# Interleaving the first two output pieces of the first batch in a fused attention and GELU-MLP kernel

## The chip, the cores and the metric

The kernel runs on one core of a Trainium2 chip, in one launch. The metric is the device time of an execution in microseconds (us); the time of a kernel is the median of its runs. The core's engines are named as in the profile: PE (TensorE, the matmuls), PEld (PE's weight loads, which run beside its matmuls), DVE (VectorE), ACT (ScalarE), POOL (GpSimd) and SP (SyncE, which here only issues DMAs). Each engine takes its own instructions in the order in which the program lists them, and an instruction that waits for another engine holds all that stand behind it on its own engine.

## The reference

Cosine attention over 8 batches of 12 heads, 448 positions and 64 dimensions a head, then an exact-GELU MLP over the 3584 rows that come out:

```python
q_n = q / (norm(q) + 1e-06);  k_n = k / (norm(k) + 1e-06)
attn = softmax(q_n @ k_n.T / tau)          # per batch and head, 448 x 448
x = (attn @ v) as rows of 12 * 64 = 768    # 3584 x 768
h = x @ w_in                               # 768 x 2048
g = 0.5 * h * (1 + erf(h / sqrt(2)))
out = g @ w_out                            # 2048 x 768, float32
```

## The kernel before

A batch (448 rows of x) passes through attention in three groups of four heads, then through the first matmul of the MLP with its GELU, and then through the second, w_out. Two batches share one tile of GELU results, `g` (128 partitions, 16 rows of the hidden dimension, 896 columns), so batch 0 gives the first three output tiles of 128 columns (t = 0, 1, 2), and batch 1 the other four. The w_out work of batch b is cut into single steps that are laid between the attention steps of batch b + 1, so that PE has matmuls while ACT computes exponentials.

**An output piece.** `second_pieces(sb, t, ni)` (L414) makes the 16 steps of one piece: output tile t, half ni (384 of the 768 columns). Step kf is "row kf" of the piece: it multiplies row kf of `g` by row kf of `w_out`, in four matmuls of 64x64x384 (L427), and adds to a pair of PSUM banks, `op{sb}_{t}_{ni}`. Row 0 takes the banks (L419); row 15 is followed by their evacuation: by a DVE reduce (L436), or, where the step is run with `AC`, by a copy on ACT (L433) and an addition on DVE (L434). The evacuation stands in DVE's order at the point of the program where row 15 is recorded.

**Two bank pairs.** `free_slot()` (L410) gives the pieces pair 2 and pair 3 in turn, and each pair is one buffer. So piece 0 takes pair 2, piece 1 pair 3, piece 2 pair 2 again; the first matmul of piece 2 therefore waits until DVE has evacuated piece 0, and the first of piece 3 until piece 1 is evacuated. Pair 2 is opened by `open_third` (L385), pair 3 by `open_fourth` (L389) in the space in which the last results of the first MLP matmul lay before; its first use waits for their GELUs on ACT.

**The order.** For the first two batches the order is written out by hand in `opening()` (L538): each line records its instructions at that place, on each engine. `more(0)` (L790) appends the steps of batch 0's six pieces to a list, sorted by ni: pieces (0,0), (1,0), (2,0), (0,1), (1,1), (2,1); below they are piece 0, 1, 2 and so on. `run(n)` (L503) takes the next n steps off that list; `run(1, AC)` takes one with evacuation by ACT. With 16 steps a piece, steps 0 to 15 of the list are piece 0, steps 16 to 31 piece 1, and step 32 is row 0 of piece 2. The lines from L796 to L812 run steps 0 to 11; then come the first scores and

```python
        run(8)                              # L815: steps 12 to 19
        run(1)                              # L821: 20
        gather(3, 1)                        # L825, DVE
        run(2)                              # L826: 21, 22
        run(2)                              # L828: 23, 24
        gather(3, 2)                        # L833, DVE
        gather(3, 3)                        # L834, DVE
        run(5)                              # L835: 25 to 29
        attend(3, 4, 0)
        scores(3, ((0, 5), (1, 5)), 1)
        run(1)                              # L838: 30
        run(1, AC)                          # L839: 31
        run(5)                              # L840: 32 to 36
```

(lines without a step, a gather or the scores ahead of step 30 are left out). `scores` (L247) are matmuls, `exps` (L261) the exponentials on ACT; `gather(g, c)` (L280) adds chunk c of the exponentials to a running sum on DVE, 128x896 in float32, and waits for the exponential of its chunk.

**The weights.** `load_wo(i)` (L471) brings rows 4i to 4i + 3 of w_out, one DMA issued by POOL each; the last two of the four, for rows 8 to 11 and 12 to 15, are issued late in `opening()` (L767, L782). The first matmul of a row that comes with a new load waits for that load.

Of the kernel before, what the change touches and what calls it, by code (L numbers as in the profile page):

```python
# [16 lines left out]
def kernel(  # L17
# [25 lines left out]
    KF = d_ff // 128  # L43
# [65 lines left out]
    def pair(i, name):  # L109
        pool = late.get(i, ps_st)  # L110
        return pool.tile([128, 2, 512], F32, tag=f"st{i}", name=name)
# [290 lines left out]
    def store(sb, t, src, c0, c1, engines):  # L402
        dst = out.rearrange("(b p c) d -> b c p d", b=B, c=C)
        for h in range(2):
            bb, c = divmod(2 * t + h, C)
            engines[h].dma_start(out=dst[2 * sb + bb, c, :, c0:c1], in_=src[64 * h:64 * (h + 1)])
# [3 lines left out]
    def free_slot():  # L410
        slot[0] ^= 1
        return slot[0]

    def second_pieces(sb, t, ni):  # L414
        state = {}

        def mm(kf, eng):
            if kf == 0:
                state["ps"] = pair(free_slot(), f"op{sb}_{t}_{ni}")  # L419
                if ni == 0:  # L420
                    ot_t[sb, t] = op_.tile([128, d_model], F32, tag="ot", name=f"ot{sb}_{t}")
            ps, ot = state["ps"], ot_t[sb, t]
            for r in range(2):
                rows = slice(64 * r, 64 * (r + 1))
                for c in range(2):
                    cols = slice(64 * c, 64 * (c + 1))
                    nc.tensor.matmul(ps[cols, r, :NH], lhsT=g_t[sb][rows, kf, t * 128 + 64 * c:t * 128 + 64 * (c + 1)],  # L427
                                     rhs=wo[rows, kf, ni * NH:(ni + 1) * NH],
                                     start=(kf == 0), stop=(kf == KF - 1), tile_position=(64 * r, 64 * c))
            if kf == KF - 1:  # L430
                part = ot[:, ni * NH:(ni + 1) * NH]
                if eng is nc.scalar:
                    nc.scalar.copy(part, ps[:, 0, :NH])  # L433
                    nc.vector.tensor_tensor(part, part, ps[:, 1, :NH], ALU.add)  # L434
                else:
                    nc.vector.tensor_reduce(part, ps[:, :, :NH].rearrange("p r d -> p d r"), mybir.AxisListType.X, ALU.add)  # L436


                if sb == B // 2 - 1 and 3 <= t < 6:
                    store(sb, t, ot[:, ni * NH:(ni + 1) * NH], ni * NH, (ni + 1) * NH, (nc.sync, nc.sync))  # L440
                elif ni == 1:
                    store(sb, t, ot, 0, d_model, (nc.sync, nc.sync))

        return [lambda eng=nc.vector, kf=kf: mm(kf, eng) for kf in range(KF)]


    def last_pieces(sb, t):
        def part(c0, c1):
            ps = pair(free_slot(), f"op{sb}_{t}_{c0}")[:, 0]
            for kf in range(KF):  # L450
                nc.tensor.matmul(ps[:, :c1 - c0], lhsT=g_t[sb][:, kf, t * 128:(t + 1) * 128], rhs=wo[:, kf, c0:c1],  # L451
                                 start=(kf == 0), stop=(kf == KF - 1))
            ot = op_.tile([128, d_model], F32, tag="ot", name=f"last{c0}")[:, :c1 - c0]
            nc.vector.tensor_copy(ot, ps[:, :c1 - c0])  # L454
            store(sb, t, ot, c0, c1, (nc.sync, nc.scalar))

        n = d_model // 6
        return [lambda c0=c0, c1=c1: part(c0, c1) for c0, c1 in ((0, 3 * n), (3 * n, 5 * n), (5 * n, 6 * n))]
# [914 lines left out]
    def output_pieces(b):  # L1373
        sb, hf = divmod(b, 2)
        todo = [(t, ni) for t in (range(3) if hf == 0 else range(3, 7)) for ni in range(2)]
        if b == 0:
            todo.sort(key=lambda x: x[1])
        tail = [2 * S // 128 - 1] if b == B - 1 else []
        fill = [f for t, ni in todo if t not in tail for f in second_pieces(sb, t, ni)]
        return fill + [f for t in tail for f in last_pieces(sb, t)]  # L1380

    def more(b):
        todo_t.extend(output_pieces(b))
# [12 lines left out]
    for b in range(3, B):  # L1396
        attention(b, output_pieces(b - 1))
        first(b)
    for f in output_pieces(B - 1):
        f()  # L1400
# [35 lines left out]
```

## Time and profile before

| what | value |
|---|---|
| median of 3 runs | 391.75 us (391.03 to 391.83) |
| span of the profiled execution, first to last instruction | 390.6 us |
| what lies around the span, against the median | 1.15 us |
| DVE busy | 273.0 us, 70% of the span |
| ACT busy | 269.9 us, 69% |
| POOL busy | 248.7 us, 64% |

The profiled execution's time is its span and what lies around it, launch and end; sums are made against the 390.6 us and then added to the median. The rows of PE, and those of the stretch that the change touches (52 to 64 us after the span's start), stand in the prediction. In a row of the timeline, the first number is when the first instruction of a merged group starts, the second the time to the end of the last, and xN how many there are; consecutive PE groups overlap a little, because matmuls are pipelined.

### The profile page before, as it was taken

How to read it: one execution, taken by the hardware profiler on the slowest of the kernel's cores; microseconds unless marked ns; L12 is line 12 of the kernel's file. 1: busy time of each engine (PE TensorE's matmuls, PEld its weight loads, DVE VectorE, ACT ScalarE, POOL GpSimd, SP SyncE). 2: the span in 40 equal slices, each digit the busy share in tenths (PEclk: the TensorE clock that was granted, in tenths of full speed). 3: DMA queues.
4: the chain of work that ended last, by engine and by line, in shares of the span. 5: the costliest groups of instructions: out<-in, count | busy, mean ns of one | idle time of the engine just before them, and what ended most of it. 6: DMA issues, size and time to landing. Idle time of an engine off the chain costs nothing.

```text
span 390.6 us, 13166 instructions
## 1 busy us (share of the span) xinstructions
PE 382.6 (98%) x5820; PEld 236.6 (61%) x5820; DVE 273.0 (70%) x509; ACT 269.9 (69%) x391; POOL 248.7 (64%) x161
## 2 busy tenths in 40 slices
PE   7899999999999999999999999999999999999996
PEld 3444568555777656865567556775567555655674
DVE  4878439876778896879696896889685993670032
ACT  5895789857999958996678767997577646504300
POOL 4796950557998399969594794969595770910000
PEclk9999999999999999999999999999999999999999
DMA  8999999926899691889067490876045600130033
GB/s 265 264 262 229 176 191 329 254 56 157 179 203 299 112 217 69 185 158 275 5 172 130 120 243 2 185 131 118 3 91 81 154 9 2 44 82 2 7 79 83
DMA packets 64473, 54.85 MB, mean 140 GB/s; under 512 B 38688, under 2 KB 60320, under 8 KB 64416
## 3 DMA queue, kind: packets, MB, share of 16 engines
q1 hardware_dynamic: 54464, 41.79, 42.0%
q0 software_dynamic: 9568, 11.80, 18.5%
q8 instruction: 45, 0.74, 0.8%
q10 hardware_dynamic: 384, 0.43, 0.4%
q14 instruction: 12, 0.10, 0.1%
HBM read 45.61 MB, written 11.01 MB: 145 GB/s over the span
## 4 chain that ended last, share of the span: by engine, by line
PE 95%; DMA 2%; SPq 1%; ACT 1%; issue 0%; DVE 0%; ACTq 0%
PE hp L493 37%; PE op L427 36%; PE st L257 9%; PE o L346 8%; DMA qk<-in_k_dram 2%; PE op L451 1%; PE sm L323 1%; PE sm L332 1%; PE tp L236 1%; SPq L134 1%; ACT sq L173 0%; ACT pt L267 0%; PE spin L489 0%; DVE last L454 0%; ACT root L195 0%
## 5 line engine op out<-in xcount | busy, mean ns | idle before, releaser
L427 PE MATMUL op<-wo,g 64*64 64x384 bf16 x3456 | 167.1, 323 | 0.2 <-issue 0.2
L267 ACT ACTIVATE pt<-st 128x896 bf16<-128x896 f32 x168 | 147.2, 918 | 19.6 <-PE st L257 17.5
L493 PE MATMUL hp<-x,wi 128*128 128x448 bf16 x768 | 147.0, 353 | 0.0
L427 PEld LDWEIGHTS <-g 64*64 64x64 bf16 x3456 | 106.2, 107 | 40.9 <-issue 4.2
L493 PEld LDWEIGHTS <-wi 128*128 128x128 bf16 x768 | 74.3, 98 | 71.6 <-issue 3.2
L219 POOL TENSOR_TENSOR qkb<-qk,rn 128x896 bf16<-128x896 f32 (+1 forms) x49 | 80.4, 1662 | 46.0 <-DVE rn L203 37.9
L278 POOL TENSOR_TENSOR acc<-acc,pt 128x896 f32<-128x896 f32 x55 | 103.8, 1888 | 4.3
L436 DVE TENSOR_REDUCE ot<-op 128x384 f32<-128x768 f32 x50 | 47.3, 946 | 54.7 <-PE op L427 47.5
L1357 ACT ACTIVATE g<-hp 128x448 bf16<-128x448 f32 x96 | 46.2, 547 | 55.1 <-PE hp L493 55.1
L257 PE MATMUL st<-qkT 64*64 64x448 bf16 x672 | 62.8, 352 | 0.5 <-ACT pt L267 0.5
L183 DVE TENSOR_REDUCE nq<-sq 128x14 f32<-128x896 f32 (+1 forms) x50 | 50.4, 1036 | 13.6 <-ACT sq L173 7.1
L380 DVE TENSOR_TENSOR x<-o,rs 128x448 bf16<-128x448 f32 x48 | 27.6, 611 | 22.9 <-PE o L346 21.9
L175 POOL TENSOR_TENSOR sq<-qk 128x896 f32<-128x896 f32 x16 | 26.6, 1685 | 23.8 <-DMA qk<-in_q_dram 13.3
L346 PE MATMUL o<-pt,v 64*64 64x448 bf16 x672 | 39.5, 349 | 0.0
L290 DVE TENSOR_TENSOR acc<-acc,pt 128x896 f32<-128x896 f32 x30 | 33.0, 1099 | 1.0
L173 ACT ACTIVATE sq<-qk 128x896 f32<-128x896 f32 (+1 forms) x33 | 28.8, 901 | 4.4 <-DMA qk<-in_q_dram 3.2
L257 PEld LDWEIGHTS <-qkT 64*64 64x64 bf16 x672 | 23.1, 106 | 11.7 <-issue 3.7
L375 DVE STREAM_TRANSPOSE rs<-rc 128x448 f32<-128x448 f32 x48 | 28.1, 621 | 0.4
L278 POOL TENSOR_TENSOR acc<-pt 128x896 f32<-128x896 bf16 x11 | 20.7, 1878 | 10.9 <-ACT pt L267 10.9
L346 PEld LDWEIGHTS <-v 64*64 64x64 bf16 x672 | 21.1, 107 | 9.2 <-issue 0.2
L522 ACT ACTIVATE g<-hp 128x448 bf16<-128x448 f32 x32 | 15.4, 547 | 12.8 <-PE hp L493 12.7
L295 DVE TRANSPOSE_TENSOR_REDUCE sa<-acc 128x28 f32<-128x896 f32 x17 | 18.8, 1104 | 0.2
(54 smaller groups left out, 176.0 us busy)
## 6 DMA issues: line engine op xcount, KB each, us to landing
qk<-in_q_dram SPq DMA_DIRECT2D x23, 448.0 KB, 4.9
qk<-in_k_dram SPq DMA_DIRECT2D x23, 448.0 KB, 5.8
out_dram<-ot SPq DMA_DIRECT2D x48, 192.0 KB, 4.0
v<-in_v_dram POOLq DMA_DIRECT2D x6, 672.0 KB, 7.2
wo<-in_moe_w_out_dram POOLq DMA_DIRECT2D x4, 768.0 KB, 10.6
wi<-in_moe_w_in_dram POOLq DMA_DIRECT2D x4, 512.0 KB, 13.8
out_dram<-ot SPq DMA_DIRECT2D x12, 96.0 KB, 2.1
wi<-in_moe_w_in_dram POOLq DMA_DIRECT2D x4, 256.0 KB, 14.1
```

The costliest lines, as they stand in the source:

```text
L173: eng.activation(sq, t, AF.Square)
L183: nc.vector.tensor_reduce(nq_t[n][:, j, i], sq_t[g, i][:, s0:s1], mybir.AxisListType.X, ALU.add)
L219: eng.tensor_tensor(qkb[:, i, :, s0:s1].rearrange("p c s d -> p s c d"), t[:, i, s0:s1], rn[:, i].to_broadcast([128, s1 - s0, C, D]), ALU. ...
L257: nc.tensor.matmul(st[cols, n, :S], lhsT=qkT[rows, 1, c, cols], rhs=qkT[rows, 0, :, cols], start=True, stop=True, tile_position=(64 * s, 6 ...
L267: nc.scalar.activation(pt, st[:, :, :S], AF.Exp, scale=inv_tau)
L278: nc.gpsimd.tensor_tensor(acc_t[g], all_t[g][:, 0] if c == 1 else acc_t[g], all_t[g][:, c], ALU.add)
L290: nc.vector.tensor_tensor(acc_t[g], acc_t[g], all_t[g][:, c], ALU.add)
L346: nc.tensor.matmul(bank_t[g, h][cols, :S], lhsT=v_t[g][rows, s, c, :], rhs=pt_t[g, s, c][rows], start=(c == 0), stop=(c == C - 1), tile_po ...
L427: nc.tensor.matmul(ps[cols, r, :NH], lhsT=g_t[sb][rows, kf, t * 128 + 64 * c:t * 128 + 64 * (c + 1)], rhs=wo[rows, kf, ni * NH:(ni + 1) * NH],
L436: nc.vector.tensor_reduce(part, ps[:, :, :NH].rearrange("p r d -> p d r"), mybir.AxisListType.X, ALU.add)
L493: nc.tensor.matmul(t, lhsT=wi[:, kd, m * 128:(m + 1) * 128], rhs=x_t[b][:, kd, :], start=(kd == 0), stop=(kd == KD - 1))
L1357: nc.scalar.activation(g_t[sb][:, m, hf * S:(hf + 1) * S], hps.pop(m), AF.Gelu)
```

## The change

In batch 0 the 32 steps of pieces 0 and 1 are put in another order: rows 0 to 11 of piece 0, rows 0 to 11 of piece 1, rows 12 to 15 of piece 0, rows 12 to 15 of piece 1. The steps of the other pieces, and all lines of `opening()`, stay. The same instructions are recorded; none is added or removed.

```diff
         tail = [2 * S // 128 - 1] if b == B - 1 else []
-        fill = [f for t, ni in todo if t not in tail for f in second_pieces(sb, t, ni)]
+        pieces = [second_pieces(sb, t, ni) for t, ni in todo if t not in tail]
+        if b == 0:
+            n = KF * 3 // 4
+            one, two = pieces[:2]
+            pieces[:2] = [one[:n] + two[:n] + one[n:] + two[n:]]
+        fill = [f for p in pieces for f in p]
         return fill + [f for t in tail for f in last_pieces(sb, t)]
```

By the list, piece 0's row 15, with its evacuation, goes from step 15 to step 27; row 12 of piece 0 from step 12 to step 24; row 0 of piece 1 from step 16 to step 12. Row 15 of piece 1 stays at step 31, and row 0 of piece 2 at step 32.

On DVE, at the end of the first MLP matmul and the start of batch 1's attention (`op_0_0` and `op_1_0` are the banks of pieces 0 and 1, `op_2_0` those of piece 2, `ot_t` the output tiles in SBUF, `acc` the running sum of `gather`, `pt` the exponentials), the order before is

```order
L241 COPY qkT_754<-tp_0_763 128x896 [waits PE_49]
L436 TENSOR_REDUCE ot_0_830<-op_0_0_829 128x384 [waits PE_49,Activation_49]
L283 TENSOR_TENSOR acc_962<-pt_939 128x896 [waits Activation_49]
L283 TENSOR_TENSOR acc_962<-acc_962,pt_939 128x896 [waits DVE_49,Activation_49] x2
L434 TENSOR_TENSOR ot_1_922<-ot_1_922,op_1_0_921 128x384 [waits Activation_49]
L283 TENSOR_TENSOR acc_962<-acc_962,pt_939 128x896 [waits DVE_49]
```

and in the change

```order
L241 COPY qkT_754<-tp_0_763 128x896 [waits PE_49]
L283 TENSOR_TENSOR acc_961<-pt_938 128x896 [waits Activation_49]
L283 TENSOR_TENSOR acc_961<-acc_961,pt_938 128x896 [waits DVE_49,Activation_49] x2
L436 TENSOR_REDUCE ot_0_830<-op_0_0_829 128x384 [waits PE_49]
L434 TENSOR_TENSOR ot_1_905<-ot_1_905,op_1_0_904 128x384 [waits Activation_49]
L283 TENSOR_TENSOR acc_961<-acc_961,pt_938 128x896 [waits DVE_49]
```

The reduce that empties piece 0's banks has moved from ahead of the first three additions of `gather` to behind them. (The numbers at the ends of names are the program's counters and mean nothing.)

On PE, behind the second scores of group 3 (step 12 of the list), the order before is

```order
L257 MATMUL st_1_899<-qkT_754 64x448
L427 LDWEIGHTS g_123
L427 MATMUL op_0_0_829<-wo,g_123 64x384 [waits DMASW5_49]
L427 LDWEIGHTS g_123
L427 MATMUL op_0_0_829<-wo,g_123 64x384
```

and in the change

```order
L257 MATMUL st_1_899<-qkT_754 64x448
L427 LDWEIGHTS g_123
L427 MATMUL op_1_0_904<-wo,g_123 64x384 [waits Activation_49]
L427 LDWEIGHTS g_123
L427 MATMUL op_1_0_904<-wo,g_123 64x384
```

The row that waits for the last load of w_out (`DMASW5_49`) has left this place, to step 24, and the first row of piece 1 with its wait for ACT has come.

On PE, where piece 2 begins (steps 31 and 32), the change has

```order
L427 MATMUL op_1_0_904<-wo,g_123 64x384
L427 LDWEIGHTS g_123
L427 MATMUL op_1_0_904<-wo,g_123 64x384
L427 LDWEIGHTS g_123
L427 MATMUL op_2_0_1035<-wo,g_123 64x384 [waits DVE_49]
```

These rows read the same before, apart from counters, and nothing moved here. The wait on DVE is for the reduce of piece 0, whose banks piece 2 takes: the count of DVE instructions that it waits for is 66 before and 69 in the change.

## The prediction

> **What bounds the kernel now.** I read the page's totals first, then its chain of work that ended last, then PE's waits from 60 us on. From the page:
>
> ```profile
> span 390.6 us, 13166 instructions
> PE 382.6 (98%) x5820; PEld 236.6 (61%) x5820; DVE 273.0 (70%) x509; ACT 269.9 (69%) x391; POOL 248.7 (64%) x161
> PE 95%; DMA 2%; SPq 1%; ACT 1%; issue 0%; DVE 0%; ACTq 0%
> ```
>
> PE is busy for 382.6 of 390.6 us and holds 95% of the chain. Its waits in the window from 60 us to the end come to one row:
>
> ```profile
> PE op L427 <- issue: 0.2, 1, 0.2
> ```
>
> So behind the place of the change PE waits for 0.2 us in all. Two things follow. Time is won only by taking away a wait of PE, of which there is almost none left; and a wait that is put in is paid in full, because no later slack of PE can take it up. The question is therefore which waits of PE the change takes out or puts in between 52 and 64 us.
>
> PE's timeline of that stretch, before:
>
> ```profile
> 51.95 2.15 PE L427 MATMUL op<-wo,g 64*64 64x384 bf16 x48
> 53.93 0.55 PE L257 MATMUL st<-qkT 64*64 64x448 bf16 x8
> 54.31 1.47 PE L427 MATMUL op<-wo,g 64*64 64x384 bf16 x32
> 55.61 0.36 PE L257 MATMUL st<-qkT 64*64 64x448 bf16 x4
> 55.80 0.66 PE L427 MATMUL op<-wo,g 64*64 64x384 bf16 x12
> 56.28 0.36 PE L257 MATMUL st<-qkT 64*64 64x448 bf16 x4
> 56.47 1.31 PE L427 MATMUL op<-wo,g 64*64 64x384 bf16 x28
> 57.61 0.57 PE L257 MATMUL st<-qkT 64*64 64x448 bf16 x8
> 57.99 1.81 PE L427 MATMUL op<-wo,g 64*64 64x384 bf16 x40
> 59.61 0.38 PE L257 MATMUL st<-qkT 64*64 64x448 bf16 x4
> 59.80 1.98 PE L427 MATMUL op<-wo,g 64*64 64x384 bf16 x44
> ```
>
> Counted in steps of four matmuls, these are steps 0 to 11, 12 to 19, 20 to 22, 23 to 29, 30 to 39 and 40 to 50. No row carries an idle time. Forty matmuls (steps 30 to 39) start between 57.99 and 59.61, so a step takes 1.62 / 10 = 0.162 us. Step 32, row 0 of piece 2, starts at 57.99 + 2 x 0.162 = **58.31 us**.
>
> **What the change removes.** Row 12 of piece 0, which waits for the last load of w_out, leaves step 12. The rows of the last two loads (in the window 40 to 60 us, and the first of the two alone, in 42.5 to 43.5 us):
>
> ```profile
> L473 POOL DMA_DIRECT2D wo<-in_moe_w_out_dram x2: 760/784/808, 42.9 to 43.7; - x2
> DMA to landing us min/median/max: 7.3/8.8/10.3
> ...
> wo<-in_moe_w_out_dram POOLq DMA_DIRECT2D x1, 768.0 KB, 7.3
> ```
>
> The first took 7.3 us to land, so the last took 10.3: 43.7 + 10.3 = 54.0 us. Step 12 starts at 54.31, and PE is not idle ahead of it. In the profiled execution the load was there 0.3 us early, and the removed wait is worth **nothing**. In a timed run it could be worth something, if the load is later there. A bound from rows: all that lies between the span (390.6) and the median (391.75) is 1.15 us, so if the profile was lucky by all of that, the change wins 1.15 us. I take zero, as the row shows it. In its new place, step 24, the row starts about 56.47 + 0.16 = 56.63, and the load has landed 2.6 us earlier.
>
> **What comes to step 12.** Row 0 of piece 1 waits for ACT, whose last GELU stands in this row:
>
> ```profile
> 49.79 2.81 ACT L522 ACTIVATE g<-hp 128x448 bf16<-128x448 f32 x6 [0.59 <-PE hp L493]
> ```
>
> It ends at 52.60, 1.7 us before step 12: no cost. ACT, POOL and SP keep their order, with the same DMAs at the same places; they cost nothing by themselves.
>
> **What moves on DVE.** Piece 0's reduce goes behind three additions of `gather`. DVE's timeline before:
>
> ```profile
> 55.25 0.96 DVE L436 TENSOR_REDUCE ot<-op 128x384 f32<-128x768 f32 x1 [6.96 <-ACT pt L267]
> 56.12 1.08 DVE L283 TENSOR_TENSOR acc<-pt 128x896 f32<-128x896 bf16 x1
> 57.31 2.29 DVE L283 TENSOR_TENSOR acc<-acc,pt 128x896 f32<-128x896 f32 x2
> 59.51 0.55 DVE L434 TENSOR_TENSOR ot<-ot,op 128x384 f32<-128x384 f32 x1
> 59.98 2.28 DVE L283 TENSOR_TENSOR acc<-acc,pt 128x896 f32<-128x896 f32 x2
> 62.17 0.55 DVE L434 TENSOR_TENSOR ot<-ot,op 128x384 f32<-128x384 f32 x1
> ```
>
> Before, the reduce lay at 55.25 to 56.21, in time in which DVE had been idle (6.96 us ahead of it), and step 32 at 58.31 found the banks free 2.1 us early. In the change:
>
> 1. Do the additions start earlier without the reduce? The first waits for the second exponential. ACT's and POOL's rows:
>
> ```profile
> 54.34 3.40 ACT L267 ACTIVATE pt<-st 128x896 bf16<-128x896 f32 x4 [0.43 <-PE st L257]
> 56.13 1.13 POOL L161 COPY then<-pt 128x1 bf16<-128x1 bf16 x1 [4.25 <-ACT pt L267]
> ```
>
> POOL's copy of the same chunk starts at 56.13, just as it is released by ACT, beside the addition at 56.12. So ACT set that time and the additions stay where they are. The third ends at 57.31 + 2.29 = 59.60.
>
> 2. The reduce starts behind it. The instruction that stood there before (L434) started at 59.51, 0.09 us ahead of the addition's end, as DVE lets a next instruction that needs nothing of it begin. From 59.51 it takes 0.96 us: until **60.47**. Were it to wait for the end as the additions wait for each other (57.31 against an end at 57.20, 0.1 us later), it would be 60.66; I take the nearer row, L434.
>
> 3. From DVE's end to PE's start: in the opening PE waits for a DVE copy, in these rows of DVE (window 10.8 to 11.1 us) and PE:
>
> ```profile
> 10.70 0.55 DVE L241 COPY qkT<-tp 64x896 bf16<-64x896 bf16 x1
> 11.31 0.35 PE L489 MATMUL spin<-g,ident 128*128 128x448 bf16 x1 [0.94 <-DVE qkT L241]
> ```
>
> The copy ends at 11.25 and PE starts at 11.31: 0.06 us. Step 32 starts at 60.47 + 0.06 = **60.53**.
>
> 4. PE's new wait: 60.53 - 58.31 = **2.2 us** (2.4 with the later start). All of steps 32 onwards, scores 6 of group 3 and all of the rest stand behind it.
>
> **Is it paid again, or paid back, behind that?** Piece 1's addition follows at about 60.4 to 60.9 (0.87 us later than before), and the fourth and fifth additions of `gather` end at about 63.1 instead of 62.26. Step 48 needs piece 1's banks: before it started at 59.80 + 8 x 0.162 = 61.1, now at 63.3, with the banks free at 60.9. Piece 2's ACT copy is released by PE and goes 2.2 us later, as does everything that PE releases; its DVE addition, 62.17 before, was held by DVE itself and comes some 1.9 us later, less than PE's shift. So DVE keeps up, nothing more is paid. And by the row of PE's waits 0.2 us is all that could be won back.
>
> The sum: 390.6 + 2.2 = 392.8 for the span, and on the median 391.75 + 2.2 = **394.0 us** (0.56%).
>
> **A rule against it.** The Trainium skill, "Perfetto Trace Analysis", section "Matmuls", says that independent matmul groups should rotate through different PSUM banks, so that evacuating one overlaps the matmuls of the next. The change fills both bank pairs to the end before either is emptied. By that rule alone the price would be the evacuation as far as it finds no matmuls beside it, the first rival below. No row of before shows the exposed case.
>
> **The rivals.**
>
> *Only the bare evacuation shows.* If the reduce began as soon as piece 0's row 15 is done, DVE being free, the wait would be small. Before, row 15 of piece 0 (step 15) started at 54.31 + 3 x 0.162 = 54.80 and the reduce at 55.25, 0.45 later. In the change it is step 27, at 56.47 + 4 x 0.162 = 57.12; reduce 57.57 to 58.53, PE at 58.59, a wait of 0.3 us: **392.0 us**. For it speaks that DVE's instruction could be ready; against it that the additions stand ahead of it in DVE's order and occupy DVE from 56.12 to 59.60.
>
> *The last load of w_out is late in the timed runs.* This is the case on the other side. Place: step 12. If the load lands later than 54.31, the kernel before waits there for the excess and the change does not. It breaks even when the load lands 2.2 us after 54.31, at 56.5, and wins from there. For it speaks the margin of only 0.3 us and a landing that differs by 3 us between two equal loads; against it that runs differ by 0.8 us in all. With the bound of 1.15 us, the time is 391.75 + 2.2 - 1.15 = **392.8 us**; at break-even 391.75.
>
> *The wait costs the clock too.* PE's rows in the opening:
>
> ```profile
> 1.95 3.52 PE L489 MATMUL spin<-g,ident 128*128 128x448 bf16 x9 [1.95 <-DVE root L93]
> 5.98 1.68 PE L489 MATMUL spin<-g,ident 128*128 128x448 bf16 x8
> ```
>
> Equal matmuls take 3.52 / 9 = 0.39 us at first and 1.68 / 8 = 0.21 later, so a slow phase of about ten matmuls costs some 10 x 0.18 = 1.8 us. If an idle 2.2 us brings it back, the time is **395.8 us**. Against it: behind the idle 0.94 us ahead of 11.31 a matmul of the same shape lasted 0.35 us in all, less than the 0.39 us by which the slow ones follow each other; but no idle time of 2.2 us is shown. The Trainium skill, "TensorE: Matmul & The Clock Gate", section "HAM oscillation — how this bites in real kernels", puts the limit at idle gaps over about 3.4 us; by that rule the clock stays, and the trace agrees as far as its 0.94 us goes.
>
> *The change doesn't do what it says:* excluded, since the order of PE and DVE shows it.
>
> **How the numbers follow.** Forecast (394.0): 0.78. Bare evacuation (392.0): 0.04. Late load: 0.05 at 392.8 or near it, 0.03 about break-even, 0.03 beyond. Clock (395.8): 0.07. A measurement of this kernel tells about 0.2%, 0.8 us, from no change. So faster is 0.03; same 0.03 + 0.04 = 0.07; slower 0.78 + 0.05 + 0.07 = 0.90. The range goes from the partly late load, 392.8, to the forecast with the later start of the reduce, 394.2, and the 0.6 us by which runs of before differed around the median: 394.8. Left out are 0.17.
>
> **What would show it.** PE's waits gain a row "op L427 <- ot L436" of some 2.2 us at about 58.3, once; DVE's reduce lies at 59.5 to 60.5, behind three additions at unchanged times; step 12 stays at 54.31; behind 61 us all PE rows lie 2.2 us later. A reduce ahead of the additions, a wait under 1 us, or a load of w_out that lands behind 54.31 in other executions of the kernel before would make this wrong; matmuls slower than 0.162 us a step behind the wait would show the clock.

## The result, and the profile after

| kernel | median of its runs | lowest to highest | profiled execution | its span |
|---|---|---|---|---|
| before | 391.60 us (8 runs) | 390.93 to 393.17 | not listed | 390.6 us |
| the change | 394.73 us (8 runs) | 392.74 to 401.12 | 395.16 us | 393.4 us |

The change is slower: its ratio to before is 1.0068, with a 95% interval of 1.0042 to 1.0093, that is 1.6 to 3.6 us. By their mean granted clock, seven of the eight runs of the change fall into two groups: 392.74, 392.97 and 394.20 us with 1.000, and 394.52, 394.94, 395.16 and 395.81 us with 0.996. The run of 401.12 us, with 0.979, is one of those executions, found with every kernel here, whose mean clock is 0.991 or less: they are left out where clear and halved executions are counted below, a few of them stand in the ratios and widen their intervals, and the three that were profiled (eight rows, the longest wait, the change again) have a half clock in the opening and the same steps some 6 to 9 us later.

The page of the change:

```profile
span 393.4 us, 13165 instructions
PE 384.2 (98%) x5820; PEld 238.0 (60%) x5820; DVE 273.1 (69%) x509; ACT 270.0 (69%) x391; POOL 248.5 (63%) x161
```

PE does the same 5820 matmuls, and is busy for 1.6 us longer. Its waits from 50 us on, with the total, how often and the longest:

```profile
PE op L427 <- DVE ot L436: 2.0, 1, 2.0
PE op L427 <- issue: 0.4, 1, 0.4
```

The first row is new: one wait of an output step for DVE's reduce. PE's timeline around it:

```profile
50.98 2.14 PE L427 MATMUL op<-wo,g 64*64 64x384 bf16 x48
52.95 0.55 PE L257 MATMUL st<-qkT 64*64 64x448 bf16 x8
53.33 1.47 PE L427 MATMUL op<-wo,g 64*64 64x384 bf16 x32
...
57.01 0.51 PE L427 MATMUL op<-wo,g 64*64 64x384 bf16 x8
59.52 2.28 PE L427 MATMUL op<-wo,g 64*64 64x384 bf16 x32 [2.00 <-DVE ot L436]
61.53 0.65 PE L257 MATMUL st<-qkT 64*64 64x448 bf16 x4
61.90 2.77 PE L427 MATMUL op<-wo,g 64*64 64x384 bf16 x44
64.48 0.57 PE L257 MATMUL st<-qkT 64*64 64x448 bf16 x8
```

Step 0 starts 0.97 us earlier than in the profile of before, since the opening happened to run faster; it varies by more than 1 us between executions. All else is read against it. Up to step 31 nothing has changed: step 12 starts at 53.33, 2.35 us behind step 0, and at 54.31 - 51.95 = 2.36 before. Step 32 would have followed at 57.01 + 0.33 = 57.34, and starts at 59.52: 2.2 us late. Behind it the matmuls themselves are slower: the 44 matmuls from 61.90 take 2.77 us, and took 1.98 before.

DVE's timeline, after:

```profile
55.12 1.09 DVE L283 TENSOR_TENSOR acc<-pt 128x896 f32<-128x896 bf16 x1 [7.81 <-ACT pt L267]
56.31 2.29 DVE L283 TENSOR_TENSOR acc<-acc,pt 128x896 f32<-128x896 f32 x2
58.52 0.95 DVE L436 TENSOR_REDUCE ot<-op 128x384 f32<-128x768 f32 x1
59.39 0.55 DVE L434 TENSOR_TENSOR ot<-ot,op 128x384 f32<-128x384 f32 x1
```

The additions start when ACT releases them, as before, and the reduce stands behind them; it ends at 59.47, and PE starts 0.05 us later.

PE's clock in stretches of 3.4 us (start and end, length, busy time, instructions, granted clock, DMA share, GB/s):

```profile
53.25:56.66 3.41, 3.41 (x92) 1.00 1.27 145
56.67:60.07 3.40, 1.40 (x36) 1.00 1.09 337
60.09:63.48 3.39, 3.39 (x48) 0.50 1.17 272
63.50:66.90 3.40, 3.40 (x88) 1.00 1.08 360
```

The stretch in which PE was idle for 2.0 us is followed by one at half clock, in which 48 matmuls start where about 90 do at full clock. Half of 3.41 us, 1.7 us, is lost there. The stretches are laid here where the trace's record of the clock changes, 60.08 and 63.49 us.

### The profile page after: what moved, and what is told of

Read it like the earlier page. It is cut to its first block, busy times and chain, and to the rows that moved or that the text cites. A ratio compares the mean times of both kernels' runs of the same rounds, so it can differ in the third digit from the quotient of the medians.

```text
span 393.4 us, 13165 instructions
## 1 busy us (share of the span) xinstructions
PE 384.2 (98%) x5820; PEld 238.0 (60%) x5820; DVE 273.1 (69%) x509; ACT 270.0 (69%) x391; POOL 248.5 (63%) x161
## 4 chain that ended last, share of the span: by engine, by line
PE 91%; DMA 4%; POOL 2%; issue 1%; DVE 1%; ACT 0%; POOLq 0%; DVEq 0%
PE hp L493 37%; PE op L427 36%; PE o L346 8%; PE st L257 7%; DMA v<-in_v_dram 4%; PE op L451 1%; POOL qkb L219 1%; DVE acc L283 1%; PE sm L332 1%; ACT pt L267 0%; PE sm L323 0%; DVE ot L436 0%; POOL v L155 0%; POOL wi L467 0%; PE tp L236 0%
## 5 line engine op out<-in xcount | busy, mean ns | idle before, releaser
L427 PEld LDWEIGHTS <-g 64*64 64x64 bf16 x3456 | 107.5, 108 | 43.3 <-issue 6.7
L346 PE MATMUL o<-pt,v 64*64 64x448 bf16 x672 | 39.5, 349 | 0.1
L346 PEld LDWEIGHTS <-v 64*64 64x64 bf16 x672 | 20.9, 107 | 9.6 <-DMA v<-in_v_dram 0.3
```

Source lines behind the costliest of these rows:

```text
L346: nc.tensor.matmul(bank_t[g, h][cols, :S], lhsT=v_t[g][rows, s, c, :], rhs=pt_t[g, s, c][rows], start=(c == 0), stop=(c == C - 1), tile_po ...
```

## The experiments

The theory: the loss is PE's wait for piece 0's reduce, 2.2 us, and in a part of the executions the half clock that this idle time brings. The first rival: the interleaved order itself costs, with two pieces open at a time. The second: the half clock has nothing to do with the wait. Each kernel was timed beside the kernel before on the same chip. "Clear" executions are those whose mean clock is 0.998 or more (the missing part lies at the end); "halved" ones have one more stretch of half clock, 0.994 to 0.996. Of the kernel before, on the four chips used, 68 executions were clear, from 390.07 to 394.81 us with a median of 391.76, and none was halved.

| kernel | PE's wait at step 32, trace | ratio to before, 95% interval | clear: number, median | halved |
|---|---|---|---|---|
| the change, two times | 2.0 us | 1.0068 (1.0042 to 1.0093); 1.0066 (1.0041 to 1.0091) | 7, 393.19 us | 6 of 13 |
| interleaved, reduce ahead | none over 0.2 us | 1.0023 (0.9989 to 1.0058) | 6, 392.09 | 0 of 6 |
| eight rows | none | 1.0042 (1.0003 to 1.0081) | 7, 392.23 | 0 of 7 |
| order of before, late reduce | 2.0 | 1.0062 (1.0035 to 1.0089) | 8, 393.50 | 1 of 9 |
| the same, behind two additions | 0.8 | 1.0011 (0.9989 to 1.0033) | 9, 392.32 | 0 of 9 |
| the same, and half a reduce more | 1.3 | 1.0048 (1.0014 to 1.0082) | 11, 392.96 | 0 of 11 |
| the same, three additions and a reduce more | 3.0 | 1.0114 (1.0088 to 1.0140) | 1, 394.98 | 4 of 5 |
| the change, seven spins | no usable trace | 1.0062 (1.0038 to 1.0086) | 7, 394.27 | 0 of 7 |
| the change, five spins | 0.5 and 0.4 | 1.0069 (1.0044 to 1.0095) | 5, 393.87 | 0 of 5 |

Where step 32 starts 2.2 us late, the table has 2.0: the trace counts as waiting only the time in which PE was idle, and the matmuls started before run until 57.01 + 0.51 = 57.52 us.

**The interleaved order with the reduce ahead of two additions.**

```diff
+        run(5)
         gather(3, 2)
         gather(3, 3)
-        run(5)
```

> The interleaved order of the change, with the second and third addition of gather recorded behind step 29 and not ahead of step 25, so that the reduce of piece 0 stands behind one addition on DVE. If the loss is the wait behind the additions (and the half clock that follows it), PE's wait ahead of step 32 falls from 2.2 to about 0.3 us, no execution shows a half clock in that stretch, and the time is within 0.7 us of the kernel before. If the interleaved order itself costs (two pieces open at a time), the time stays about 2 to 3 us above before, without a wait at step 32.

The clear executions lie 0.3 us above before, none is halved. DVE now takes the reduce behind one addition (its timeline, and PE's of the same execution):

```profile
54.74 1.09 DVE L283 TENSOR_TENSOR acc<-pt 128x896 f32<-128x896 bf16 x1 [7.81 <-ACT pt L267]
56.15 0.96 DVE L436 TENSOR_REDUCE ot<-op 128x384 f32<-128x768 f32 x1 [0.32 <-PE op L427]
57.03 2.28 DVE L283 TENSOR_TENSOR acc<-acc,pt 128x896 f32<-128x896 f32 x2
```

```profile
56.63 2.02 PE L427 MATMUL op<-wo,g 64*64 64x384 bf16 x40
...
66.00 1.14 PE L346 MATMUL o<-pt,v 64*64 64x448 bf16 x20 [0.40 <-DVE ot L434]
```

and the last of these rows in the kernel before:

```profile
66.37 1.14 PE L346 MATMUL o<-pt,v 64*64 64x448 bf16 x20
```

Steps 30 to 39 now run through, in 2.02 us against 1.81: the bare evacuation costs 0.2 us, and step 32 starts at 56.63 + 0.33 + 0.2 = 57.16. What I had not reckoned with comes later: DVE's additions are some 0.9 us late against PE, and the first matmul of `values(3)`, which needs the banks of piece 3, waits for DVE. That matmul starts 66.00 - 57.16 = 8.8 us behind step 32 here, and started 66.37 - 58.31 = 8.1 us behind it before. So by its trace the order costs 0.2 + 0.8 = 1.0 us, by its six clear executions 0.3; the openings differ by more than that between them. What it costs, it costs through DVE's lag, not through matmuls that have become slower.

**Eight rows and not twelve.**

```diff
-            n = KF * 3 // 4
+            n = KF // 2
```

> The change with eight rows of each piece ahead and not twelve: rows 0 to 7 of piece 0, rows 0 to 7 of piece 1, rows 8 to 15 of each. Piece 0 then ends at step 23, ahead of the second addition of gather, and its reduce stands behind one addition on DVE. If the wait is the cause, PE does not wait ahead of step 32 (the reduce ends at about 58.1 us, 0.2 us before it is needed), and the time is that of before within 0.3 us, clock 1.000. If the interleaving itself costs, it is 2 us or more above before.

PE does not wait ahead of step 32, as expected; the clear executions are 0.5 us above before, not within 0.3, for the same reason as in the experiment above (PE's waits hold "o L346 <- DVE ot L434", 0.4 us).

**The reduce alone moved, in the order of before.** The evacuation of piece 0 is kept back and recorded at another place; PE's order is that of before.

```diff
+            if kf == KF - 1 and (sb, t, ni) == (0, 0, 0):
+                held.append(lambda: nc.vector.tensor_reduce(
+                    ot[:, :NH], ps[:, :, :NH].rearrange("p r d -> p d r"), mybir.AxisListType.X, ALU.add))
+                return
...
         gather(3, 2)
         gather(3, 3)
+        held.pop()()
         run(5)
```

> The order of the kernel before on PE, with only the reduce of piece 0 recorded behind three additions of gather, as in the change. If the wait for that reduce is the cause, this does what the change does: PE waits 2.2 us ahead of step 32, about half of the executions show a granted clock of 0.5 for 3.4 us behind it and take 1.7 us more, and the median is some 2 to 4 us above before. If the interleaving is the cause, the time is that of before.

Without any interleaving, the loss is there: 1.0062 against 1.0068 and 1.0066, with intervals that cover each other. PE's timeline, and the stretches around it:

```profile
56.34 0.52 PE L429 MATMUL op<-wo,g 64*64 64x384 bf16 x8
58.86 1.48 PE L429 MATMUL op<-wo,g 64*64 64x384 bf16 x20 [2.00 <-DVE ot L433]
```

```profile
55.85:59.24 3.39, 1.39 (x36) 1.00 1.01 260
59.26:62.66 3.40, 3.40 (x48) 0.50 1.15 272
```

The wait is the same to 0.01 us. One of nine executions was halved, fewer than "about half"; with so few, 1 of 9 and 6 of 13 do not tell two shares apart.

**Shorter and longer waits.** The held reduce behind two additions:

```diff
         gather(3, 2)
+        held.pop()()
         gather(3, 3)
```

> The order of the kernel before on PE, with the reduce of piece 0 recorded behind two additions of gather: PE's wait ahead of step 32 should be about 59.3 - 58.3 = 1.0 us. If the half clock comes from idle time that fills more than about half of a stretch of 3.4 us, no execution has it (clock 1.000 in all) and the time is 1.0 us above before. If any idle time of PE can bring it, or chance, some executions show a clock of 0.996 and lie 1.7 us higher than the others.

Behind two additions and a DVE reduce of half the size, whose result is unused:

```diff
         gather(3, 2)
+        idle = nrm.tile([128, 14], F32, tag="idle", name="idle", bufs=1)
+        nc.vector.tensor_reduce(idle, all_t[3][:, 0, 0].rearrange("p (b r) -> p b r", r=32), mybir.AxisListType.X, ALU.add)
+        held.pop()()
         gather(3, 3)
```

> The order of the kernel before on PE, with the reduce of piece 0 behind two additions of gather and one more DVE reduce of about 0.5 us, whose result is unused: a wait of about 1.5 us ahead of step 32, between the 1.0 us that showed no half clock and the 2.2 us that showed it in a part of the executions. If more than about half of a stretch of 3.4 us has to be idle, none has it and the time is 1.5 us above before. If the share only grows with the idle time, some do.

Behind three additions and a reduce of that kind over twice the columns (1.08 us):

```diff
         gather(3, 2)
         gather(3, 3)
+        idle = nrm.tile([128, 28], F32, tag="idle", name="idle", bufs=1)
+        nc.vector.tensor_reduce(idle, all_t[3][:, 0].rearrange("p s (b r) -> p (s b) r", r=32), mybir.AxisListType.X, ALU.add)
+        held.pop()()
         run(5)
```

> As the late reduce alone (the order of before on PE), with one more DVE reduce of about 1 us, whose result is unused, ahead of piece 0's reduce: PE's wait ahead of step 32 should be about 3.2 us. If the half clock comes when idle time fills more than about half of a stretch of 3.4 us, wherever the stretch begins, nearly all executions (9 in 10) have it, clock 0.996, and the time is 3.2 + 1.7 = 4.9 us above before. If its share is the same as with the wait of 2.2 us, about half of them do.

Step 32 in the three traces, in this order:

```profile
59.31 1.01 PE L429 MATMUL op<-wo,g 64*64 64x384 bf16 x20 [0.81 <-DVE ot L433]
59.43 0.84 PE L429 MATMUL op<-wo,g 64*64 64x384 bf16 x16 [1.33 <-DVE ot L433]
66.24 2.12 PE L429 MATMUL op<-wo,g 64*64 64x384 bf16 x24 [2.99 <-DVE ot L433]
```

The steps came as wanted: it starts 1.0, 1.5 and 3.2 us behind its expected start. Clear executions rise with the wait, but with the two shorter waits only by 0.6 and 1.2 us, where 1.0 and 1.5 were expected. None of these 20 is halved; with the longest wait 4 of 5 are, and those have a median of 396.62 us, 4.9 us above before, as forecast. In the longest wait's trace, PE is busy for 0.40 of a stretch of 3.39 us, and the next is halved:

```profile
62.90:66.29 3.39, 0.40 (x15) 1.00 1.13 349
66.31:69.70 3.39, 3.39 (x44) 0.50 1.16 278
```

With the wait of 1.5 us, 1.33 us of a stretch were idle, and the clock stayed (the stretches around the wait):

```profile
57.57:60.97 3.40, 2.07 (x52) 1.00 1.16 296
60.99:64.40 3.41, 3.41 (x89) 1.00 1.15 289
```

**The change with PE kept busy in the wait.** First seven, then five idle matmuls (128x128x448, results unused) ahead of step 32:

```diff
         run(1, AC)
+        keep = pair(0, "keep")
+        for _ in range(5):
+            nc.tensor.matmul(keep[:, 0, :S], lhsT=ident, rhs=blank, start=True, stop=True)
         run(5)
```

> The change with seven idle matmuls (128x128x448, results unused) on PE ahead of step 32, in the time in which it waits; they take the banks of scores 4 and so start when its exponential is done, about 0.7 us into the wait. If idle time of PE brings the half clock, it is gone in all executions (clock 1.000) and the time is the wait alone, 2.2 us above before. If the half clock is from something else (the DMAs or the load of that stretch), it stays in about half of them and the median is again about 3 us above before.

> The change with five idle matmuls (128x128x448, results unused) on PE in the wait. The wait stays at about 2.2 us from the end of step 31 to step 32, but PE's idle time in it is cut in two pieces of some 0.7 and 0.4 us. If idle time is the cause of the half clock, no execution has it, while the change itself beside it has it in a third or more; the median is then 2.2 us above before. If not, the shares are alike.

None of the twelve executions counted is halved. With five, step 32 stays where the reduce lets it start:

```profile
56.68 0.51 PE L427 MATMUL op<-wo,g 64*64 64x384 bf16 x8
57.68 1.11 PE L842 MATMUL keep<-g,ident 128*128 128x448 bf16 x5 [0.49 <-ACT pt L267]
59.19 1.49 PE L427 MATMUL op<-wo,g 64*64 64x384 bf16 x32 [0.41 <-DVE ot L436]
```

From 57.01, where step 32 would have started, to 59.19 are 2.2 us, and the median is 2.1 us above before: the wait's price without the half clock. With seven it is 2.5 us; its trace is of an execution with a span of 1030.9 us, in which PE was slow from the first matmul to the last, and says nothing about the wait. The spins kept the clock, but the ratios, 1.0062 and 1.0069, are not below the change's 1.0068 and 1.0066: a gain in time is not shown.

**The change again**, beside those two.

> The change as it is, on the same chip as the next two, so that the share of executions with the half clock can be compared: a wait of 2.2 us ahead of step 32 in the profile, and between a third and two thirds of the executions with one stretch of 3.4 us at a clock of 0.5 behind it, which lie 1.7 us above the rest.

The wait is 2.00 us once more, and two of six executions were halved. Its profiled execution was not halved here, and shows why a part escapes (stretches laid by the clock's last change in that trace, at 27.01 us):

```profile
61.15:64.55 3.40, 2.90 (x72) 1.00 1.36 160
64.57:67.96 3.39, 1.91 (x48) 1.00 1.10 326
67.98:71.37 3.39, 3.39 (x92) 1.00 1.14 298
```

The same 2.0 us of idle time lie across a border: 0.50 in one stretch, 1.49 in the next.

**A late load of w_out.** The last load is issued behind `load_v(2)`, once in the order of before, once with the interleaved order and the reduce ahead (the first experiment).

```diff
         gelu(0, 15)
-        load_wo(3)
...
         load_v(2)
+        load_wo(3)
         run(3)
```

> The kernel before with the last load of w_out issued later on POOL, behind the load of v (about 3 us later). If step 12 has only 0.3 us to spare, PE waits there for the load, by about 2 to 3 us, and a half clock can follow. If the load's place in POOL's queue does not set when it lands, there is no wait.

> The interleaved order with the reduce of piece 0 behind one addition (the first experiment), with the same later load. Row 12 of piece 0 now stands at step 24, some 2.3 us behind step 12, so the wait for the load should be gone or below 0.7 us: about 2 us less than the kernel before with the late load. If the interleaving has no use even then, the two are equal.

In the order of before, PE waits for the load at step 12, and a half clock follows there too (timeline and stretches):

```profile
53.49 0.55 PE L257 MATMUL st<-qkT 64*64 64x448 bf16 x8
56.76 1.75 PE L427 MATMUL op<-wo,g 64*64 64x384 bf16 x17 [2.72 <-DMA wo<-in_moe_w_out_dram]
```

```profile
53.04:56.43 3.39, 1.00 (x24) 1.00 1.23 97
56.45:59.84 3.39, 3.08 (x40) 0.50 1.26 258
```

In the interleaved order PE does not wait for the load, though it lands behind step 12 there as well: issued at 45.2 us, it takes 8.9 us to land, so until 54.1; step 12 starts at 52.74 and step 24, the first to need it, at 54.90 + 0.16 = 55.06.

```profile
wo<-in_moe_w_out_dram POOLq DMA_DIRECT2D x1, 768.0 KB, 8.9
52.74 1.47 PE L427 MATMUL op<-wo,g 64*64 64x384 bf16 x32
54.90 1.31 PE L427 MATMUL op<-wo,g 64*64 64x384 bf16 x28
```

But the times do not tell the two apart: 1.0006 (0.9969 to 1.0042) of before against 0.9985 (0.9951 to 1.0020). The clear executions of the first lie between 390.80 and 394.63 us, six in number, so in some the load seems to have come in time; their waits were not traced. That the interleaving removes a wait for a late load is shown by the two traces; how much it is worth is left open.

## Why the prediction was right, and where its sizes were off

**The wait.** All four steps of its sum held. The additions stayed where ACT puts them; the reduce started 0.08 us ahead of the third addition's end (58.52 against 56.31 + 2.29 = 58.60), as the nearer row said; it took 0.95 us; PE followed 0.05 us later. The wait was forecast as 2.2 us and is 2.2 us (57.34 to 59.52). The late reduce alone makes the same wait, so the reduce's place on DVE is what makes it, and not the interleaving on PE. The prediction's rival of the bare evacuation was rightly held unlikely: it takes another order on DVE, as the experiment with the reduce ahead shows (0.2 us there, 0.3 worked out).

**The removed wait was nothing.** In the profile of the change PE runs into step 12 without idle time, as before. The late load in the timed runs had a bound of 1.15 us, "all that lies between the span and the median". That bound was mis-sized: what lies around the span is 395.16 - 393.4 = 1.8 us in the change, and 1.7 to 1.9 us in every run that lists both. By that, the profiled execution of before would have stood at 392.4 us: slower than the median, and not a lucky one. The forecast was not moved by it, since it was added to the median.

**Paid back.** Up to 0.2 us was allowed for. Clear executions of the change lie 1.4 us above before, of the late reduce 1.7, of the five spins 2.1, where the wait is 2.2; the two shorter waits fell short too, by 0.4 and 0.3 us. The traces show no such gain: from step 32 to the last instruction are 390.6 - 58.31 = 332.3 us before, and in the seven traces that wait ahead of step 32 they are 331.4 to 332.9 (less 1.7 us where a halved stretch follows), with a mean of 332.3. With 5 to 11 executions a kernel, which spread by 1.4 to 2.5 us, and an opening that varies by more than 1 us, whether the timed runs win back more than 0.2 us stays open.

**The clock was the term that was mis-sized.** The rival "the wait costs the clock too" was priced at 1.8 us and given 0.07. The price was right: 1.7 us in the trace, and halved executions of the change have a median of 394.96 us against 393.19. The chance was not: 6 of 13 executions have it. It is not one case or the other but both, from one execution to the next, and the measured median of 394.73 us, 0.7 above the forecast, lies where the two groups mix. What failed was the argument against this rival: it rested on a gap of 0.94 us, which can't tell what one of 2.2 us does. The Trainium skill, "TensorE: Matmul & The Clock Gate", section "HAM oscillation — how this bites in real kernels", puts the limit at idle gaps over about 3.4 us. That pointed the wrong way: here 2.0 us in a stretch was enough. The Trainium skill, "TensorE: Matmul & The Clock Gate", section "What's actually happening", says that the window is free-running and 3413 ns long. With that the traces agree: the stretches at half clock last 3.41 us, and the same 2.0 us of idle time lie whole in one stretch in two traces, and across a border, unpunished, in a third.

How often that happens can be estimated from these two lengths. If a border may fall anywhere, 2.0 us of idle time lie whole in one stretch in (3.41 - 2.0) / 3.41 = 0.41 of the executions; of 3.0 us, 2.0 or more lie in one stretch in (0.41 + 2 x 1.0) / 3.41 = 0.71. If less than 2.0 us is enough, both shares are higher. Counted were 6 of 13 and 1 of 9, and 4 of 5, too few to test the estimate closely.

**Luck.** Neither group of executions has its median at the forecast of 394.0: that of the clear ones lies 0.8 us below it, that of the halved ones 1.0 above. That the median over all came so near is owed to their mixture. The range owed its upper end, 394.8, to 0.6 us for the spread of the runs of before, which the three runs listed don't show: they lie 0.72 us below to 0.08 above their median. With 0.08 in its place the range would have ended at 394.3, below the measured 394.73.

**The experiments' second rival**, that the half clock has nothing to do with the wait, fell: 0 of 68 executions of before, 0 of 12 with spins in the wait and 0 of 20 with 1.3 us of idle time or less are halved, against 7 of 22 with 2.0 us and 4 of 5 with 3.0.

## What to carry to other kernels

Before steps are reordered on the bound engine, look where the instruction that frees their buffer comes to stand on the engine that frees it: here the matmuls merely changed places, and the loss came from a 0.96 us reduce that slid behind 3.4 us of additions in DVE's order. A wait of PE that takes 2.0 us or more of a clock stretch of 3.4 us can cost another 1.7 us, so a median over executions is a mixture; read the granted clock of each run beside its time, and take differences from executions with the same clock. Where such a wait can't be removed, a few idle matmuls in it kept the clock in all twelve executions counted here, though the time was not shown to fall by it.

## What the runs showed of the hardware

The half clock follows a stretch of 3.41 us in which PE was idle for 2.0 us or more (2.0 in two traces, 2.4 and 3.0 in one each), and behind the opening it did not follow idle times of 1.49 us or less (four traces: 0.8, 1.3, 1.49, and the spins' two short ones). Where between 1.5 and 2.0 us the limit lies wasn't tried. Each time one stretch was halved; PE was busy in it for 3.08 us or more, and the next was full again.

In the opening, less idle time was enough. In the profile of the change again, PE's busy time in the last stretch before the clock fell was

```profile
9.95:13.35 3.40, 1.89 (x20) 1.00 1.17 297
13.37:27.00 13.63, 13.63 (x77) 0.50 1.09 257
```

and the clock stayed at a half for four stretches, though PE counts as busy in them. In the profile of the longest wait the last stretch before the fall was

```profile
8.28:11.68 3.40, 1.97 (x20) 1.00 1.09 342
```

Behind the opening, 1.91 us busy had been enough to keep the clock. The matmuls of these stretches of the opening are mostly small transposes (128x128); whether those count for less was not tried.

One execution, of the change with seven spins, had a span of 1030.9 us: by its profile's page a w_out matmul lasted 679 ns on average where it lasts 323 in the kernel before, from the first to the last. It came once in all these runs, and its cause is open.
